# A fused spectral-attention and feed-forward kernel: the order of three steps in the first chunk, and ten of 48 weight blocks converted during attention

## The chip, the cores and the metric

The kernel runs on one core of one Trainium2 chip, as a single program. The metric is device time in microseconds (us), the median of several executions; beside it stands one execution recorded by the hardware profiler. Five engines work side by side, each with its own queue in order: TensorE (PE), VectorE (DVE), ScalarE (ACT), GpSimd (POOL) and SyncE (SP), which here issues all transfers.

## The reference

Sigmoid attention over 8 batches, 12 heads, 448 positions and 64 channels, then a spectral mix and a feed-forward block:

```python
scores = scale * np.matmul(q, k.transpose(0, 1, 3, 2)) - np.log(S)
attn = 1.0 / (1.0 + np.exp(-scores))
x = np.matmul(attn, v)                      # (8, 448, 768) after regrouping the heads
mixed = np.real(np.fft.fft(np.fft.fft(x, axis=1), axis=2)).astype(np.float32)
u = x + mixed
un = (u - mu) / np.sqrt(var + 1e-06)        # mean and variance of each row of u
ch = np.maximum(un @ w_ch1, 0.0) @ w_ch2    # 768 -> 3072 -> 768
return (u + ch).astype(np.float32)
```

The two weight matrices arrive as float64. The kernel sees each number as two 32-bit words, a low and a high one.

## The kernel before

**Stages.** First comes attention with the spectral mix: 48 groups of four steps, 192 steps in all, which the loop from L518 takes two at a time, with a tail of a few more. Then the feed-forward block runs over seven chunks of 512 rows: chunk 0 and chunk 1 in the plain way (`up_proj`, `evac` and `down_proj`, L554 to L584), five more by a scheme with fewer multiplications, whose weights chunk 1 prepares (`combine`).

**Order.** The order of instructions on each engine is written out by hand. `pin()` (L453) chains every instruction to the one before it on the same engine, so each engine works strictly in the order in which the program issues.

**One iteration of attention** (two steps) issues: postponed small operations, two `scores` (PE, then the sigmoid on ACT), two `values` (PE; every fourth one ends with `xT`, DVE's copy out of PSUM), some units of the spectral mix on PE, and then, step by step, whatever `at(t, fn)` has filed under that step, in the order of filing. Filed are the folds of `xT` (on POOL, some on DVE), the loads of q, k and v, `cast` (POOL, L117) and `rest` (DVE, L122), which split q and k in two parts for the scores two iterations later, and the row normalisation `norm`. A group g has its `cast` at step 4g-4 and its `rest` at step 4g-3.

**The weights during attention.** The 48 blocks of the weights (24 of `w1`, 24 of `w2`, each 128 x 768 numbers, 768 KB) pass through once: `weight_load(n)` brings block n into one of three `wr` buffers, and `weight_max(n)` (L264, DVE) takes the largest magnitude. `when_w` holds the step of each block: block n at step 14 + n*156//48. At step 170 `weight_scales` makes the two scale factors `wsc` from them.

**The weights in the first chunk.** Each block is loaded again and prepared in five steps (`prep_w(i, f, n)`, `i` for the matrix, `f` for the block):

- n = 0: the load, 768 KB from `w_in`, into a `wr` buffer or one of two `spare` buffers (L389)
- n = 1: `Abs` of the high word, as float32, into `t`, a `wt` buffer (ACT, L398)
- n = 2: clamp (L400) and shift (L402), DVE
- n = 3: two ORs (L406 takes bits of the low word, L408 the sign) finish the float32 number in `t`, DVE; then `h`, the scaled high part in float16 (the copy, ACT, L416), and a store of `t` to `t_dram` (SP, L417), from where chunk 1's `combine` reads it
- n = 4: `l`, the low part, `t*scale - h` in float16 (DVE, L419)

`order` lists the blocks: three of `w1`, then one of `w2` and one of `w1` by turns; from block 6 on an even place is a `w1` block and an odd one a `w2` block. `prep_step(k, n)` is one quarter of slot k. Its four quarters issue: the loads that `loadable` allows and **the low part of block k-1**; `Abs` of block k+1; clamp and shift of block k; the ORs, the copy and the store of block k. In chunk 0 every f has two slots (6+2f and 7+2f), until slot 48 is through. Its order in the program:

```python
up_proj(c, f)                 # PE: 18 matmuls, 512 columns
...                           # first slot: four quarters of prep_step
evac(c, f)                    # ACT: hh = relu(psh), L567;  DVE: hl, L568
...                           # second slot
down_proj(*prev)              # PE: the f before, from its hh and hl
```

`psh`, `hh` and `hl` have two buffers each. The first blocks are prepared at the end of attention, three more slots while the last units of the mix run.

Of the kernel before, what the change touches and what calls it, by code (L numbers as in the profile page):

```python
# [9 lines left out]
F32 = mybir.dt.float32  # L10
F32R = mybir.dt.float32r
I32 = mybir.dt.int32
AF = mybir.ActivationFunctionType
ALU = mybir.AluOpType
# [9 lines left out]
DM = 768  # L24
# [3 lines left out]
NFC = DF // 128  # L28
# [26 lines left out]
HI_MIN = 1.125 * 2.0 ** -15  # L55
HI_MAX = 2.0 ** 16 * 1.875 - 2.0 ** -7


def spectral_attention_ffn(tc, q, k, v, w1, w2, cd, cs, ident_in, out):
    nc = tc.nc  # L60
# [7 lines left out]
    with ExitStack() as top:  # L68
# [3 lines left out]
        t_dram = dram.tile([2, NP, 128, 2, DM], F32, name="t_dram")  # L72
# [8 lines left out]
        wpre = top.enter_context(tc.tile_pool(name="wpre", bufs=1))  # L81
# [6 lines left out]
        if True:  # L88
# [164 lines left out]
            wtile = {}  # L253
# [8 lines left out]
            def weight_max(n):  # L262
# [2 lines left out]
                    out=wmax[:, i, f:f + 1], in_=wtile.pop(n)[:, :, 1].bitcast(F32), op=ALU.max, axis=AX.X,  # L265
                    apply_absolute_value=True)

            def weight_scales():
                wm = cpool.tile([128, 2], F32, name="wm")
                nc.vector.tensor_reduce(out=wm, in_=wmax, op=ALU.max, axis=AX.X)  # L270
                ws = cpool.tile([128, 4], F32, name="ws")
                nc.gpsimd.partition_all_reduce(ws[:, 0:2], wm, 128, bass_isa.ReduceOp.absmax)

                wi = ws.bitcast(I32)
                nc.vector.tensor_scalar(
                    out=wi[:, 0:2], in0=wi[:, 0:2], scalar1=20, scalar2=0x7FF,
                    op0=ALU.logical_shift_right, op1=ALU.bitwise_and)
                nc.vector.tensor_scalar(
                    out=wi[:, 0:2], in0=wi[:, 0:2], scalar1=1023 - 60, scalar2=1023 + 60, op0=ALU.max, op1=ALU.min)
                nc.vector.tensor_scalar(  # L280
                    out=wi[:, 0:2], in0=wi[:, 0:2], scalar1=-896, scalar2=1 << 23, op0=ALU.add, op1=ALU.mult)
                nc.vector.reciprocal(ws[:, 2:4], ws[:, 0:2])
                nc.vector.tensor_scalar(
                    out=wsc[:, 0:1], in0=ws[:, 2:3], scalar1=2.0 ** 3, scalar2=None, op0=ALU.mult)
                nc.vector.tensor_scalar(
                    out=wsc[:, 1:2], in0=ws[:, 3:4], scalar1=2.0 ** 11, scalar2=None, op0=ALU.mult)
                nc.vector.tensor_scalar(
                    out=wsc[:, 2:3], in0=ws[:, 0:1], scalar1=ws[:, 1:2],
                    scalar2=2.0 ** -14 / UN_SCALE, op0=ALU.mult, op1=ALU.mult)
# [72 lines left out]
                return sorted(res, key=lambda x: x[0])  # L362

            prep = {}
            order = [(0, f) for f in range(NPRE)]
            for f in range(NFC):
                order += [(1, f)] + [(0, f + NPRE)] * (f + NPRE < NFC)
# [3 lines left out]
            def in_spare(k):  # L371
                return k >= 8 and k % 5 > 2

            def loadable(k, done):

                here = [j for j in range(k) if in_spare(j) == in_spare(k)]
                n = 2 if in_spare(k) else 3
                return len(here) < n or here[-n] < done

            def prep_w(i, f, n):  # L380

                if n == 0:
                    k = order.index((i, f))
                    if in_spare(k):
                        r = spare[0][:, k % 5 - 3]
                    else:
                        r = wpre.tile([128, DM, 2], I32, tag="wr", name="wr", bufs=3)
                    prep[i, f] = r
                    nc.sync.dma_start(  # L389
                        r.rearrange("p n w -> p (n w)"), (w1, w2)[i][:, f * 2 * DM:(f + 1) * 2 * DM])  # L390
                    return
                if n == 1:
                    prep[i, f] = prep[i, f], wpre.tile([128, DM], F32, tag="wt", name="wt", bufs=3)
                r, t = prep[i, f]
                ti = t.bitcast(I32)
                lo, hi = r[:, :, 0], r[:, :, 1]
                if n == 1:
                    nc.scalar.activation(t, hi.bitcast(F32), AF.Abs)  # L398
                elif n == 2:
                    nc.vector.tensor_scalar(  # L400
                        out=t, in0=t, scalar1=HI_MIN, scalar2=HI_MAX, op0=ALU.max, op1=ALU.min)
                    nc.vector.tensor_scalar(  # L402
                        out=ti, in0=ti, scalar1=3, scalar2=0x3FFFFFF8,
                        op0=ALU.logical_shift_left, op1=ALU.bitwise_and)
                elif n == 3:
                    nc.vector.scalar_tensor_tensor(  # L406
                        out=ti, in0=lo, scalar=29, in1=ti, op0=ALU.logical_shift_right, op1=ALU.bitwise_or)
                    nc.vector.scalar_tensor_tensor(  # L408
                        out=ti, in0=hi, scalar=-0x40000000, in1=ti, op0=ALU.bitwise_and, op1=ALU.bitwise_or)
                if n >= 3:  # L410
                    h, l = (x[f] for x in ((w1h, w1l), (w2h, w2l))[i])
                    if i == 0:
                        h, l = (x.rearrange("p c f -> p (c f)") for x in (h, l))
                    sc = wsc[:, i:i + 1]
                if n == 3:
                    nc.scalar.activation(h, t, AF.Copy, scale=sc)  # L416
                    nc.sync.dma_start(t_dram[i, f // 2][:, 1 - f % 2], t)  # L417
                elif n == 4:
                    nc.vector.scalar_tensor_tensor(  # L419
                        out=l, in0=t, scalar=sc, in1=h, op0=ALU.mult, op1=ALU.subtract)  # L420

            def prep_step(k, n):

                loads = []
                for d in range(2, 5):
                    if not loadable(k + d, k):
                        break
                    loads.append((d, 0))
                for d, m in ((*loads, (-1, 4)), ((1, 1),), ((0, 2),), ((0, 3),))[n]:
                    if k + d < len(order) and (k + d, m) not in prepped:  # L430
                        prepped.add((k + d, m))
                        prep_w(*order[k + d], m)
# [47 lines left out]
            when_w = {}  # L480
# [3 lines left out]

            def at(t, fn):
                extra.setdefault(t, []).append(fn)

            for b in range(B):
                for r, when in enumerate(FOLDS):
                    for n, t in enumerate(when):  # L490
                        e = nc.vector if r == 2 and n % 2 else nc.gpsimd
                        at(24 * b + LAG + t, lambda b=b, r=r, n=n, e=e: fold(b, r, n, e))
                at(24 * b + 27 + LAG, lambda b=b: units.extend(mix_units(b)))
            for gg in range(2, GG):
                at(8 * gg - 8 + LAG, lambda n=gg: load_v(n))
# [7 lines left out]
            at(9, lambda: nc.sync.dma_start(ident, ident_in))  # L503
            at(10, lambda: weight_load(1))
            at(TP, weight_scales)
            prepped = set()
            for e in range(NPRE + 2):
                for n, d in enumerate((0, 5, 6, 7, 9)):
                    if TP + 4 * e + d < TQ + LAG + 2 and (n < 4 or e < NPRE) and (n == 0 or e < NPRE + (n == 1)):
                        prepped.add((e, n))  # L510
                        at(TP + 4 * e + d, lambda e=e, n=n: prep_w(*order[e], n))
# [29 lines left out]
        with ExitStack() as fast, ExitStack() as st, ExitStack() as early:  # L541
# [72 lines left out]
            slot, step, m = NPRE, 0, 0  # L614
            while units or act_next or dve_next or sp_next:
                mix_rest(0.65)
                if len(units) < MIX_UP and m < NCC:
                    up_proj(0, 1, range(m, m + 1))
                    m += 1
                n = step % MIX_STEP  # L620
                if n < 4 and slot < NPRE + 2 * NW2:
                    prep_step(slot, n)
                    slot += n == 3
                step += 1
                pin()
# [99 lines left out]
            for j in range(NFC):  # L725
                f = 1 + j - (j > 4) - (j > 8) - (j > 12) - (j > 16)
# [168 lines left out]
            for c in range(NPLAIN + 1, NCK):  # L895
                t = (c - NPLAIN - 1) * NQ * NU
# [3 lines left out]
            for g in range(NGR):  # L900
                t = g * NU
# [81 lines left out]
```

## Time and profile before

| what | us |
|---|---|
| median of 3 runs | 1801.37 |
| lowest and highest run | 1796.43, 1805.48 |
| the profiled execution | 1796.9 |
| its span in the profile | 1795.1 |
| PE busy, all in all | 1671.5 |
| DVE busy | 1290.0 |
| ACT busy | 602.4 |
| POOL busy | 194.3 |

Attention takes the time to about 450 us, the end of the mix and chunk 0's blocks that to 718 us, chunk 0 and chunk 1 together that to about 945 us, and the five other chunks the rest. A row of a group reads: line, engine, operation, result <- inputs, shape, xcount | busy us, mean ns of one | idle us of the engine just before, and who ended it. A row of the timeline gives start, length and the instruction, with the idle time before it in brackets. `<-ACT hh L567` says that the engine waited until ACT had written `hh`.

### The profile page before, as it was taken

To read this page: it belongs to the slowest core of one execution; us is meant where nothing else is said; L and a number is where in the kernel's file an instruction comes from. 1 tells how busy PE (TensorE), PEld (TensorE's weight loads), DVE (VectorE), ACT (ScalarE), POOL (GpSimd) and SP (SyncE) were. 2 spreads that over 40 slices of the span, in tenths; PEclk is the share of its full clock that TensorE was granted. 3 is DMA by queue.
4 is the path that set the end of the run, shared out by engine and by line. 5 is a ranking of instruction groups with operands and counts; after the bars stand their busy time and mean duration, and the time that the engine had idled before them with its cause. 6 is when DMAs were issued, how large, how long until landed. Compare 5 with 4: busy or idle time off the path is not lost. (4 is left out here: it accounts for less than half of the span.)

```text
span 1795.1 us, 27673 instructions
## 1 busy us (share of the span) xinstructions
PE 1671.5 (93%) x10996; PEld 1070.2 (60%) x10996; DVE 1290.0 (72%) x2481; ACT 602.4 (34%) x767; POOL 194.3 (11%) x220
## 2 busy tenths in 40 slices
PE   8999999987878777999799999999999999999997
PEld 3555555543533333545357777777777777777774
DVE  3545577656777777467755888888888887888668
ACT  4444444434333333123232322333233323233221
POOL 4434444334000000000000000000000000000000
PEclk9999999998988999999999999999999999999999
DMA  7666767654666664587887466656475656566561
GB/s 234 209 213 211 237 208 240 212 177 118 225 211 211 211 211 140 192 307 278 302 288 271 186 247 234 238 214 242 175 277 206 237 199 254 215 229 241 216 227 59
DMA packets 109139, 394.95 MB, mean 220 GB/s; under 512 B 23521, under 2 KB 49362, under 8 KB 93522
## 3 DMA queue, kind: packets, MB, share of 16 engines
q1 hardware_dynamic: 109010, 393.19, 62.2%
q8 instruction: 86, 1.41, 0.3%
q14 instruction: 43, 0.35, 0.1%
HBM read 316.08 MB, written 73.92 MB: 217 GB/s over the span
## 5 line engine op out<-in xcount | busy, mean ns | idle before, releaser
L841 PE MATMUL pso<-ws,H 128*128 128x384 f16 x2520 | 422.6, 326 | 0.9 <-DVE H L796 0.8
L790 PE MATMUL psf<-ut,ws 128*128 128x256 f16 x3780 | 422.1, 273 | 1.1 <-DVE ur L600 1.1
L790 PEld LDWEIGHTS <-ws 128*128 128x128 f16 x3780 | 369.9, 98 | 50.3 <-issue 1.4
L841 PEld LDWEIGHTS <-H 128*128 128x128 f16 x2520 | 246.4, 98 | 155.8 <-DVE H L796 1.1
L136 ACT ACTIVATE a<-sc 112x900 f32<-112x900 f32 x192 | 166.6, 917 | 156.3 <-PE sc L132 156.1
L850 DVE TENSOR_TENSOR acc<-pso,acc 128x384 f32<-128x384 f32 x350 | 181.9, 550 | 19.0 <-PE pso L841 19.0
L579 PE MATMUL po<-w2h,hh 128*128 128x512 f16 (+1 forms) x384 | 133.7, 348 | 55.5 <-ACT hh L567 54.8
L152 PE MATMUL av<-a,vr 112*64 112x450 f32 x768 | 172.9, 573 | 3.7 <-DVE xT L161 3.7
L815 ACT ACTIVATE F<-F 128x1024 f32<-128x1024 f32 x60 | 63.5, 1058 | 332.0 <-DVE F L796 332.0
L796 DVE TENSOR_TENSOR H<-F,H 128x1024 f16<-128x1024 f32 x120 | 129.5, 1087 | 46.8 <-ACT H L825 46.8
L560 PE MATMUL psh<-ut,w1h 128*128 128x512 f16 x504 | 151.1, 382 | 5.0 <-DVE hl L568 5.0
L579 PEld LDWEIGHTS <-hh 128*128 128x128 f16 x768 | 77.5, 103 | 114.7 <-ACT hh L567 66.0
L579 PE MATMUL po<-w2h,hl 128*128 128x512 f16 (+1 forms) x384 | 132.9, 346 | 3.8 <-DVE hl L568 1.5
L796 DVE TENSOR_TENSOR F<-X,psf 128x256 f32<-128x256 f32 x240 | 98.0, 418 | 51.1 <-PE psf L790 48.1
L579 PE MATMUL po<-w2l,hh 128*128 128x512 f16 (+1 forms) x384 | 133.0, 346 | 0.0
L161 DVE TENSOR_SCALAR xT<-av 128x450 f32<-128x450 f32 x48 | 30.1, 626 | 141.8 <-PE av L152 141.8
L825 ACT ACTIVATE H<-F 128x1792 f16<-128x1792 f32 x60 | 101.8, 1697 | 89.0 <-DVE F L796 89.0
L796 DVE TENSOR_TENSOR F<-F 128x256 f32<-128x256 f32 x240 | 91.2, 421 | 17.7 <-ACT F L815 13.7
L568 DVE SCALAR_TENSOR_TENSOR hl<-psh,hh 128x512 f16<-128x512 f32 x48 | 33.2, 691 | 98.2 <-ACT hh L567 98.1
L132 PE MATMUL sc<-qh,kh 64*112 64x450 f32 x384 | 82.1, 423 | 19.7 <-ACT a L136 10.3
L152 PEld LDWEIGHTS av<-a,vr 112*64 112x64 f32 x768 | 47.8, 139 | 82.9 <-issue 68.3
L560 PE MATMUL psh<-ut,w1l 128*128 128x512 f16 x252 | 96.2, 382 | 0.0
(92 smaller groups left out, 1954.2 us busy)
## 6 DMA issues: line engine op xcount, KB each, us to landing
ws<-w_dram SPq DMA_DIRECT2D x120, 1344.0 KB, 5.9
wr<-w_in SPq DMA_DIRECT2D x80, 768.0 KB, 4.7
t_dram<-wt SPq DMA_DIRECT2D x48, 384.0 KB, 2.3
cb<-t_dram SPq DMA_DIRECT2D x24, 768.0 KB, 5.5
spare<-w_in SPq DMA_DIRECT2D x16, 768.0 KB, 4.6
qr<-q_in SPq DMA_DIRECT2D x48, 225.0 KB, 3.8
kr<-k_in SPq DMA_DIRECT2D x48, 224.0 KB, 3.5
vr<-v_in SPq DMA_DIRECT2D x24, 448.0 KB
```

What stands on the lines that cost most here:

```text
L132: nc.tensor.matmul(ps[:CP, j, :SQ], split[g, 1, kn][h, c * CP:(c + 1) * CP], split[g, 0, qn][h], start=(n == 0), stop=(n == 2))
L136: nc.scalar.activation(a, ps[:CP, :, :SQ], AF.Sigmoid, bias=-math.log(S), scale=1.0 / math.sqrt(D))
L152: nc.tensor.matmul(ps[j * D:(j + 1) * D, :SQ], vr[:, c, h * D:(h + 1) * D], a[:, j], start=(c == 0), stop=(c == 3))
L560: nc.tensor.matmul(hs[c, f], l[f][:, m], r[:, m], start=(m == n == 0), stop=(m == NCC - 1 and n == 2))
L568: nc.vector.scalar_tensor_tensor(out=hl, in0=ps, scalar=0.0, in1=hh, op0=ALU.max, op1=ALU.subtract)
L579: nc.tensor.matmul(po[n][:, at:at + hi - lo], l[:, cols], r[f][:, lo:hi], start=(f == 0 and m == 0 and at == 0), stop=(f == NFC - 1 and m ...
L790: nc.tensor.matmul(ps[:, :TH], w[:, x, a, m * 128:(m + 1) * 128], ut[y][:, b, m], start=(m == n == 0), stop=(m == n == 2))
L796: nc.vector.tensor_tensor(out=o, in0=x, in1=y, op=op)
L815: nc.scalar.activation(F[:, 0:4], F[:, 0:4], AF.Relu)
L825: nc.scalar.activation(hts[P][:, 0], F[:, 1:8], AF.Copy)
L841: nc.tensor.matmul(ps[:, :384], H[:, x, a, tp * 128:(tp + 1) * 128], w[:, y, b], start=(j == n == 0), stop=(j == 1 and n == 2))
L850: later(0, lambda: nc.vector.tensor_tensor(out=to, in0=ps[:, :384], in1=to, op=ALU.add))
```

## The change

The first part moves `(-1, 4)`, the low part of block k-1, from the first quarter of slot k to the third, behind clamp and shift of block k. The second part takes ten blocks (`ready`: `w1` blocks 7, 11, 15, 19, 23 and `w2` blocks 5, 9, 13, 17, 21) through `Abs`, clamp, shift and ORs during attention, in the three steps from the one in which their maximum is taken, and stores the float32 result in `t_dram`. In chunk 0 such a block is loaded from `t_dram` (384 KB) into the front of its buffer, and only the copy and the low part are left. As the low part of a ready block reads the loaded buffer itself, `loadable` counts that buffer as free one slot later, and `prep_step` looks for loads from one block ahead on instead of two. The ready blocks stand at the places 12 and 13, 20 and 21, 28 and 29, 36 and 37, 44 and 45 of `order`.

```diff
+            def to_float32(r, t, n):
+                ti = t.bitcast(I32)
+                lo, hi = r[:, :, 0], r[:, :, 1]
+                if n == 1:
+                    nc.scalar.activation(t, hi.bitcast(F32), AF.Abs)
+                elif n == 2:
...
+            def convert(n, k):
+                i, f = divmod(n, NFC)
+                if k == 1:
+                    made32[n] = wtile[n], wpre.tile([128, DM], F32, tag="wt", name="t32", bufs=3)
+                to_float32(*made32[n], k)
+                if k == 3:
+                    nc.sync.dma_start(t_dram[i, f // 2][:, 1 - f % 2], made32.pop(n)[1])
...
+            ready = {(i, f) for i in range(2) for f in range(7 - 2 * i, NFC, 4)}
...
-                return len(here) < n or here[-n] < done
+                return len(here) < n or here[-n] < done - (order[here[-n]] in ready)
...
+                    if (i, f) in ready:
+                        prep[i, f] = None, r.rearrange("p n w -> p (n w)")[:, :DM].bitcast(F32)
+                        nc.sync.dma_start(prep[i, f][1], t_dram[i, f // 2][:, 1 - f % 2])
+                        return
...
-                if n == 1:
+                if n == 1 and (i, f) not in ready:
...
+                if n < 4 and (i, f) not in ready:
+                    to_float32(r, t, n)
...
-                    nc.sync.dma_start(t_dram[i, f // 2][:, 1 - f % 2], t)
+                    if (i, f) not in ready:
+                        nc.sync.dma_start(t_dram[i, f // 2][:, 1 - f % 2], t)
...
-                for d in range(2, 5):
-                    if not loadable(k + d, k):
+                for d in range(1, 5):
+                    if k + d < len(order) and (k + d, 0) not in prepped and not loadable(k + d, k):
                         break
                     loads.append((d, 0))
-                for d, m in ((*loads, (-1, 4)), ((1, 1),), ((0, 2),), ((0, 3),))[n]:
+                for d, m in (loads, ((1, 1),), ((0, 2), (-1, 4)), ((0, 3),))[n]:
...
+            for t, x in when_w.items():
+                for n in x:
+                    if divmod(n, NFC) in ready:
+                        for j in range(3):
+                            at(t + j, lambda n=n, j=j: convert(n, j + 1))
```

The last loop stands ahead of the other `at` calls, so within a step the conversion is issued first. The body of `to_float32` is the arithmetic of n = 1 to 3 of `prep_w`, unchanged.

More of the change, by code (lines that the diff above doesn't have):

```diff
@@ L266, in weight_max @@
                     apply_absolute_value=True)
+            def to_float32(r, t, n):
[4 more added lines that the diff above has]
+                elif n == 2:
+                    nc.vector.tensor_scalar(
+                        out=t, in0=t, scalar1=HI_MIN, scalar2=HI_MAX, op0=ALU.max, op1=ALU.min)
+                    nc.vector.tensor_scalar(
+                        out=ti, in0=ti, scalar1=3, scalar2=0x3FFFFFF8,
+                        op0=ALU.logical_shift_left, op1=ALU.bitwise_and)
+                else:
+                    nc.vector.scalar_tensor_tensor(
+                        out=ti, in0=lo, scalar=29, in1=ti, op0=ALU.logical_shift_right, op1=ALU.bitwise_or)
+                    nc.vector.scalar_tensor_tensor(
+                        out=ti, in0=hi, scalar=-0x40000000, in1=ti, op0=ALU.bitwise_and, op1=ALU.bitwise_or)
+            def convert(n, k):
[5 more added lines that the diff above has]
+                    nc.sync.dma_start(t_dram[i, f // 2][:, 1 - f % 2], made32.pop(n)[1])
+            made32 = {}
             def weight_scales():
@@ L391, in prep_w @@
                     return
-                if n == 1:
+                if n == 1 and (i, f) not in ready:
                     prep[i, f] = prep[i, f], wpre.tile([128, DM], F32, tag="wt", name="wt", bufs=3)
                 r, t = prep[i, f]
[L395 to L409, printed above, removed]
+                if n < 4 and (i, f) not in ready:
+                    to_float32(r, t, n)
                 if n >= 3:
```

## The prediction

> **What bounds the kernel now.** First the page: its span and the engines' busy shares in 40 slices of 44.9 us.
>
> ```profile
> span 1795.1 us, 27673 instructions
> PE   8999999987878777999799999999999999999997
> DVE  3545577656777777467755888888888887888668
> ```
>
> TensorE (PE) is full nearly everywhere except in the slices from about 400 to 720 us, where it shows 7 to 8 tenths. Three windows (PE, weight loads, DVE, ACT and POOL busy, then clock, DMA share and rate): attention, the first chunk, and what follows it.
>
> ```profile
> 36.00:445.00 409.00, 376.11 (x2246) 206.79 (x2244) 245.30 (x410) 178.59 (x226) 180.30 (x200) 0.97 0.64 207
> 500.00:718.00 218.00, 173.17 (x829) 82.61 (x828) 165.61 (x215) 75.45 (x96) 0.00 (x0) 0.93 0.58 195
> 719.00:760.00 41.00, 41.00 (x223) 21.59 (x221) 16.26 (x30) 6.73 (x8) 0.00 (x0) 1.00 0.52 188
> ```
>
> Attention is PE's: 376 of 409 us. In the first chunk nobody is full: PE 173 of 218, DVE 166. So the waits of that window come next.
>
> ```profile
> PE po L579 <- ACT hh L567: 42.8, 19, 3.0
> DVE hl L568 <- ACT hh L567: 28.2, 19, 1.5
> DVE w2l L419 <- ACT w2h L416: 20.1, 20, 1.1
> ```
>
> PE waits for `hh`, the evacuation of `psh`; DVE waits for ACT in two places, once per f each. One f in order of time, DVE and then ACT, shows a closed loop of the two:
>
> ```profile
> 571.79 1.02 DVE L419 SCALAR_TENSOR_TENSOR w2l<-wt,wsc,w2h 128x768 f16<-128x768 f32 x1 [1.00 <-ACT w2h L416]
> 572.72 0.56 DVE L400 TENSOR_SCALAR wt<-wt 128x768 f32<-128x768 f32 x1
> 573.31 0.56 DVE L402 TENSOR_SCALAR wt<-wt 128x768 int32<-128x768 int32 x1
> 573.91 0.96 DVE L406 SCALAR_TENSOR_TENSOR wt<-wr,wt 128x768 int32<-128x768 int32 x1
> 574.90 0.96 DVE L408 SCALAR_TENSOR_TENSOR wt<-wr,wt 128x768 int32<-128x768 int32 x1
> 577.35 0.69 DVE L568 SCALAR_TENSOR_TENSOR hl<-psh,hh 128x512 f16<-128x512 f32 x1 [1.49 <-ACT hh L567]
> 577.95 1.01 DVE L419 SCALAR_TENSOR_TENSOR w1l<-wt,wsc,w1h 128x768 f16<-128x768 f32 x1
> ...
> 583.02 1.02 DVE L419 SCALAR_TENSOR_TENSOR w2l<-wt,wsc,w2h 128x768 f16<-128x768 f32 x1 [1.00 <-ACT w2h L416]
> ```
>
> ```profile
> 575.90 0.93 ACT L416 ACTIVATE w1h<-wt,wsc 128x768 f16<-128x768 f32 x1 [3.33 <-DVE wt L408]
> 576.74 0.58 ACT L567 ACTIVATE hh<-psh 128x512 f16<-128x512 f32 x1
> 577.21 0.90 ACT L398 ACTIVATE wt<-spare 128x768 f32<-128x768 f32 x1
> ```
>
> A block costs DVE 4.07 us from start to end: low 0.93, clamp 0.59, shift 0.60, the two ORs 0.99 and 0.96. An f is two blocks, `hl` (0.60), 1.49 us until copy and `hh` are through, and 1.00 us until the other copy is: 8.14 + 0.60 + 1.49 + 1.00 = 11.23, which is 583.02 - 571.79. PE needs less, as the `hl` rows after the last block show:
>
> ```profile
> 728.75 0.69 DVE L568 SCALAR_TENSOR_TENSOR hl<-psh,hh 128x512 f16<-128x512 f32 x1 [7.03 <-ACT hh L567]
> 736.54 0.69 DVE L568 SCALAR_TENSOR_TENSOR hl<-psh,hh 128x512 f16<-128x512 f32 x1 [7.09 <-ACT hh L567]
> ```
>
> 7.79 us for an f: while blocks are prepared, 3.44 us of each f are DVE's, and what is taken off the loop comes off the kernel.
>
> **The low part moved.** It stands behind the next block's clamp and shift (1.19 us), so the copy (0.03 + 0.93) is done when DVE reaches it. The clamp needs that block's Abs, which ACT issued ahead of the copy (572.72 follows at once today). How many waits there are:
>
> ```profile
> L419 DVE SCALAR_TENSOR_TENSOR w2l<-wt,wsc,w2h 128x768 f16<-128x768 f32 x24 | 24.4, 1018 | 22.2 <-ACT w2h L416 22.1
> L419 DVE SCALAR_TENSOR_TENSOR w1l<-wt,wsc,w1h 128x768 f16<-128x768 f32 x21 | 21.2, 1008 | 1.0 <-ACT w1h L416 1.0
> ```
>
> Some 23 of 1.0 us. The last block has no successor and keeps its wait; ten belong to the ready pairs below; **12 x 1.0 = 12.0 us** go. The 1.49 us before `hl` stay: copy and `hh` still come after the ORs.
>
> **Ready blocks.** In `order` they are 12 and 13, 20 and 21, up to 44 and 45: both blocks of one f, five times. From the end of block 11's ORs to the end of block 14's DVE spends now 1.00 + 4.07 + 1.49 + 0.60 + 4.07 + 1.00 + 4.07 = 16.30. After: low 11 waits 1.00 for its copy (nothing is left to stand before it) and takes 0.93; `hl` starts at 0.03 + 0.84 + 0.84 + 0.58 + 0.03 = 2.32, as two copies and `hh` are in line on ACT; then `hl` 0.60, low 12 0.93, clamp and shift of 14 1.19, low 13 0.93, ORs 1.95: 7.92. **8.38 saved, five times: 41.9 us.** Next bound: the two `hl` intervals of a pair are 6.99 and 7.09, under PE's 7.79, so PE falls 1.5 us behind; the plain f's at 11.23 - 1.00 = 10.23 let it catch up 2.44 each. After the last pair the blocks are soon at their end, and about 1.4 of PE's lag stays: -1.4. **Chunk: 12.0 + 41.9 - 1.4 = 52.5 us.**
>
> Transfers there:
>
> ```profile
> wr<-w_in SPq DMA_DIRECT2D x80, 768.0 KB, 4.7
> t_dram<-wt SPq DMA_DIRECT2D x48, 384.0 KB, 2.3
> ```
>
> Ten loads halve and ten stores leave the chunk. A ready block's buffer is released one slot later (its low part reads it), so its successor is loaded later. The tightest is block 16: loaded in slot 12, right after block 11's store, with its Abs behind block 14's copy, which starts 7.9 us after those ORs: 8 us against 4.7. I cost it at nothing; without that cover it is at most the 4.7 us, five times.
>
> **What attention gets.** Ten times an Abs (0.90, ACT), clamp, shift and ORs (3.14, DVE), a store. DVE has room, and PE a reserve on the short path, `rest` to the scores that read `kl`:
>
> ```profile
> L161 DVE TENSOR_SCALAR xT<-av 128x450 f32<-128x450 f32 x39 | 24.4, 627 | 116.7 <-PE av L152 116.7
> 167.74 0.98 DVE L122 TENSOR_TENSOR kl<-kr,kh 128x448 fp32r<-128x448 f32 x1
> 171.56 0.46 PE L132 MATMUL sc<-qh,kh 64*112 64x450 f32 x2
> ```
>
> Before each `xT` DVE idles 3.0 us on average, and `kl` is 2.84 us early. But the conversions stand first in their slots. Slots 36, 88, 108, 160 put clamp and shift ahead of `rest`, 62 and 134 the ORs, 75 and 147 all four, 49 and 121 none. And these operations are longer while POOL works, as the three blocks turned at the end of attention show:
>
> ```profile
> 403.72 1.22 DVE L402 TENSOR_SCALAR wt<-wt 128x768 int32<-128x768 int32 x1
> 406.79 1.30 DVE L406 SCALAR_TENSOR_TENSOR wt<-wr,wt 128x768 int32<-128x768 int32 x1
> 408.13 1.62 DVE L408 SCALAR_TENSOR_TENSOR wt<-wr,wt 128x768 int32<-128x768 int32 x1
> ```
>
> With a clamp of 0.55 that block took 4.69 us. So: two blocks overrun the reserve by 4.69 - 2.84, 3.7 us; at slot 109 clamp and shift (1.8 stretched) delay `norm`'s scaling, whose ACT copy precedes two sigmoids, where PE waits already:
>
> ```profile
> 243.99 0.46 PE L132 MATMUL sc<-qh,kh 64*112 64x450 f32 x2 [0.60 <-ACT a L136]
> ```
>
> and 0.2 for each of the other seven: **7 us**. Bounds: 0, as work is only added, and 56 (ten times 4.69 + 0.90, all on the path); I stay near the reserve's row. On SP a store waits for the ORs; behind it stand the `kr`, `qr` and weight loads, needed five slots later, so nothing.
>
> The Trainium skill (SBUF — State Buffer, "Who interferes with whom") says more: a DVE instruction with two SBUF inputs, or in a two-port mode, and a GpSimd one that reads SBUF exclude each other for the whole instruction. The stretched rows agree, and the rule speaks against the move, from a stage without POOL work to one with 180 us of it; the rival "POOL in the way" is what it would make.
>
> **Sum.** Against the profiled execution (1796.9, span 1795.1): 1796.9 - 52.5 + 7.0 = 1751.4. The median of the runs is 4.5 above it, so 1801.4 - 45.5 = **1755.9**.
>
> **Rivals.**
> - *POOL in the way* (0.15). If each of the four operations is held as 403.72 was (0.66 longer), a block takes 5.8 us, and every one overruns: 10 x (5.8 - 2.84) = 30 us at most, 15 if half do: 1763.9 to 1778.9. For it: the stretched rows. Against: five of ten put two operations or none in the way.
> - *PE's clock* (0.10). PE was slow after a gap of 2.97 us, and not after 1.40:
>
> ```profile
> 577.37 0.39 PE L579 MATMUL po<-w2h,hh 128*128 128x512 f16 x1 [2.97 <-ACT hh L567]
> 578.09 0.61 PE L579 MATMUL po<-w2h,hl 128*128 128x512 f16 x1
> 588.59 0.39 PE L579 MATMUL po<-w2h,hh 128*128 128x512 f16 x1 [1.40 <-ACT hh L567]
> 589.32 0.39 PE L579 MATMUL po<-w2h,hl 128*128 128x512 f16 x1
> ```
>
>  If PE stays busy 173 us in what are then 218 - 52.5 = 165.5, it becomes the bound: 7.7 lost, 1763.6. Gaps of at most 2.44 speak against it.
> - *The wait only moves* (0.05): the clamp waits for Abs, or the low part still for the copy. The 12.0 don't come: 1767.9.
> - *Attention becomes DVE's* (0.03), slower than before: each conversion stops PE for its stretched 4.69 + 0.90, and its ORs hold POOL, which casts the next q and k, for another 1.9: 75 - 52.5 = 22 us, 1824. It decides from 5.25 us per block. DVE's 245 of 409 us, 292 with ten blocks, speak against it.
>
> The forecast has 0.67. Its own range is 1741 (no cost in attention, and the fastest run, 1796.4) to 1766 (twice the cost, slower runs); with half of the first rival the range is **1741 to 1776**. About 9 us (0.5%) is what a measurement here can tell from no change: faster 0.96, same 0.02, slower 0.02.
>
> **What would show it.** L419's waits in all drop from 24 us to about 7; five pairs of `hl` 7 us apart among others at 10.2; blocks end near 672 instead of 718 us; four conversion rows per block between 75 and 360 us, with PE idle under 1 us behind most. Wrong if PE idles over 2 us behind several conversions, if the copy of a ready block waits for its load, or if the plain f's stay at 11.2.

## The result, and the profile after

| | before | after |
|---|---|---|
| median, us | 1798.9 (four runs, 1791.77 to 1805.48) | 1745.91 (four runs, 1744.19 to 1746.7) |
| the profiled execution | 1796.9 | 1746.7 |

The ratio is 0.9705, with a 95% interval of 0.9665 to 0.9745: 53 us by the medians, 50.2 by the profiled executions. The forecast was 1755.9, 45.5 less than before.

The page of the changed kernel, span and busy shares in 40 slices, now of 43.6 us:

```profile
span 1744.9 us, 27688 instructions
PE   8999999997879999998899999999999999999997
DVE  4556677866788884768557888788878888887768
```

The run of 7s and 8s on PE has shrunk to a few slices. Attention and the first chunk as windows (PE, weight loads, DVE, ACT, POOL, then clock, DMA share, rate):

```profile
36.00:445.00 409.00, 375.86 (x2220) 205.80 (x2216) 281.62 (x446) 182.02 (x231) 183.39 (x196) 0.97 0.67 213
500.00:655.00 155.00, 147.41 (x760) 74.53 (x761) 127.26 (x168) 64.69 (x84) 0.00 (x0) 0.97 0.67 225
```

In attention DVE has 36.3 us more than before (245.30) and PE the same; in the chunk PE is 95% busy instead of 79%. Three of the chunk's waits (500 to 665 us: waiter, awaited, us, times, longest; ACT's waits for DVE's ORs, the other side of the loop, are left out):

```profile
DVE hl L597 <- ACT hh L596: 23.7, 20, 1.5
PE po L608 <- ACT hh L596: 11.7, 5, 5.1
DVE w2l L442 <- ACT w2h L438: 6.0, 6, 1.0
```

The wait of `w2l` fell from some 20 us to 6.0 in six cases: five pairs and the last block. `hl`'s wait of 1.49 stays. One pair and the f after it, DVE in order of time:

```profile
543.66 0.69 DVE L597 SCALAR_TENSOR_TENSOR hl<-psh,hh 128x512 f16<-128x512 f32 x1 [1.49 <-ACT hh L596]
544.26 0.55 DVE L275 TENSOR_SCALAR wt<-wt 128x768 f32<-128x768 f32 x1
544.85 0.56 DVE L277 TENSOR_SCALAR wt<-wt 128x768 int32<-128x768 int32 x1
545.32 1.01 DVE L442 SCALAR_TENSOR_TENSOR w1l<-wt,wsc,w1h 128x768 f16<-128x768 f32 x1
546.25 0.95 DVE L281 SCALAR_TENSOR_TENSOR wt<-spare,wt 128x768 int32<-128x768 int32 x1
547.24 0.96 DVE L283 SCALAR_TENSOR_TENSOR wt<-spare,wt 128x768 int32<-128x768 int32 x1
549.20 1.02 DVE L442 SCALAR_TENSOR_TENSOR w2l<-wt,wsc,w2h 128x768 f16<-128x768 f32 x1 [1.00 <-ACT w2h L438]
550.50 0.69 DVE L597 SCALAR_TENSOR_TENSOR hl<-psh,hh 128x512 f16<-128x512 f32 x1 [0.29 <-ACT hh L596]
551.11 1.01 DVE L442 SCALAR_TENSOR_TENSOR w1l<-wr,wsc,w1h 128x768 f16<-128x768 f32 x1
552.04 0.55 DVE L275 TENSOR_SCALAR wt<-wt 128x768 f32<-128x768 f32 x1
552.63 0.56 DVE L277 TENSOR_SCALAR wt<-wt 128x768 int32<-128x768 int32 x1
553.10 1.01 DVE L442 SCALAR_TENSOR_TENSOR w2l<-wr,wsc,w2h 128x768 f16<-128x768 f32 x1
554.03 0.95 DVE L281 SCALAR_TENSOR_TENSOR wt<-wr,wt 128x768 int32<-128x768 int32 x1
555.02 0.96 DVE L283 SCALAR_TENSOR_TENSOR wt<-wr,wt 128x768 int32<-128x768 int32 x1
557.46 0.69 DVE L597 SCALAR_TENSOR_TENSOR hl<-psh,hh 128x512 f16<-128x512 f32 x1 [1.49 <-ACT hh L596]
```

The reader sees the forecast's picture: low 11 (549.20) keeps its 1.00, `hl` finds `hh` 0.29 us away, low 12, clamp, shift, low 13 and the ORs follow without a gap. From the last OR of block 11 to that of block 14 it is 555.02 - 547.24 = 7.78 us (forecast 7.92, before 16.30). The pair's two `hl` intervals are 6.84 and 6.96; between plain f's the trace has 9.90 to 9.91.

Where the 50.2 us went is read from rows that both traces have: the first `hl` of chunk 0, the last low part, and an `hl` behind the last block (728.75 before, in the prediction). Before:

```profile
463.15 0.69 DVE L568 SCALAR_TENSOR_TENSOR hl<-psh,hh 128x512 f16<-128x512 f32 x1 [1.63 <-ACT hh L567]
717.70 1.02 DVE L419 SCALAR_TENSOR_TENSOR w2l<-wt,wsc,w2h 128x768 f16<-128x768 f32 x1 [1.00 <-ACT w2h L416]
```

After:

```profile
466.36 0.69 DVE L597 SCALAR_TENSOR_TENSOR hl<-psh,hh 128x512 f16<-128x512 f32 x1 [1.62 <-ACT hh L596]
663.84 1.02 DVE L442 SCALAR_TENSOR_TENSOR w2l<-wt,wsc,w2h 128x768 f16<-128x768 f32 x1 [1.00 <-ACT w2h L438]
678.47 0.69 DVE L597 SCALAR_TENSOR_TENSOR hl<-psh,hh 128x512 f16<-128x512 f32 x1 [7.03 <-ACT hh L596]
```

| | forecast | measured |
|---|---|---|
| up to the first `hl` | +7.0 | 466.36 - 463.15 = +3.2 |
| the chunk, from there to the `hl` behind the last block | -52.5 | (678.47 - 466.36) - (728.75 - 463.15) = -53.5 |
| from there to the end | 0 | +0.1 |

### The profile page after: what moved, and what is told of

Same layout as the page of the kernel before. It is cut to its first block, busy times and chain, and to the rows that moved or that the text cites. A ratio compares the mean times of both kernels' runs of the same rounds, so it can differ in the third digit from the quotient of the medians.

```text
span 1744.9 us, 27688 instructions
## 1 busy us (share of the span) xinstructions
PE 1659.8 (95%) x10996; PEld 1070.3 (61%) x10996; DVE 1296.0 (74%) x2481; ACT 601.7 (34%) x767; POOL 201.8 (12%) x220
## 5 line engine op out<-in xcount | busy, mean ns | idle before, releaser
L608 PE MATMUL po<-w2h,hh 128*128 128x512 f16 (+1 forms) x384 | 128.9, 336 | 19.0 <-ACT hh L596 16.3
L608 PE MATMUL po<-w2h,hl 128*128 128x512 f16 (+1 forms) x384 | 128.5, 335 | 1.0
L608 PE MATMUL po<-w2l,hh 128*128 128x512 f16 (+1 forms) x384 | 128.5, 335 | 0.0
```

What stands on the lines that cost most here:

```text
L608: nc.tensor.matmul(po[n][:, at:at + hi - lo], l[:, cols], r[f][:, lo:hi], start=(f == 0 and m == 0 and at == 0), stop=(f == NFC - 1 and m ...
```

## The experiments

All start from the changed kernel; ratios are to the kernel before on the same chip. The theory: the chunk is the closed loop of DVE and ACT, both parts shorten it, and attention pays a few us. The main rivals: attention's price is much larger and hidden in the sum, or one of the two parts gives nothing.

**The low part alone** (`e1_low`): no ready blocks and no conversions.

```diff
-            ready = {(i, f) for i in range(2) for f in range(7 - 2 * i, NFC, 4)}
+            ready = set()
```

> The first part of the change alone: the low part behind the next block's clamp and shift, no ready blocks. Loop theory (the first chunk is set by DVE and ACT in turn, so whatever leaves that loop leaves the kernel): an f takes 9.91 us, as the plain f's of the changed kernel do, instead of 11.23, 21 times, so 28 us less than before, about 1771. By the price on record alone (1.00 us for each of 22 waits): 22 us less, 1777. Rival, the wait only moves: under 8 us less, above 1791. Attention stays as it was; its cold-clock windows (half of PE's clock) come or do not come without any conversion.

Measured: 1768.95 us, ratio 0.9837 (0.9802 to 0.9873), 27.2 us less than before. Two of its chunk's waits (500 to 690 us):

```profile
DVE hl L597 <- ACT hh L596: 28.2, 19, 1.5
PE po L608 <- ACT hh L596: 25.1, 16, 1.7
```

No wait of a low part is left but the last block's, and every f takes 9.90 to 9.91 us, 1.32 less than 11.23: the wait of 1.00, and 0.32 that the forecast didn't have.

**The ready blocks alone** (`e2_ready`): the low part at its old place, first in its slot.

```diff
-                for d, m in (loads, ((1, 1),), ((0, 2), (-1, 4)), ((0, 3),))[n]:
+                for d, m in ((*loads, (-1, 4)), ((1, 1),), ((0, 2),), ((0, 3),))[n]:
```

> The second part alone: ten ready blocks, the low part first in its slot as before. Loop theory: plain f's stay at 11.23, a pair of hl intervals takes about 15 (one more wait of 1.00 than in the changed kernel); 40 us less in the chunk, some 3 to 6 back in attention: 1762 to 1766. Both savings together would then be 28 + 40 = 68 against 53.5 in the changed kernel: ten of the waits are counted twice, and PE is the bound at the end. Rival, ready blocks do nearly all of it: within 5 us of the changed kernel, below 1751.

Measured: 1764.36, ratio 0.982 (0.979 to 0.985), 31.8 less; in its profile the span is 37.3 less. The low part waits as before the change, once for each `w2` block that is prepared in the chunk (500 to 680 us):

```profile
DVE w2l L442 <- ACT w2h L438: 15.1, 15, 1.1
```

Plain f's are at 11.22 to 11.23, pairs at 6.98 + 7.17. From landmarks in the traces the parts alone give 27.6 and 39.0 us in the chunk, 66.6 together; the whole change gives 53.5. The difference of 13.1 is overlap. 12.2 of it are there at the last low part: ten of the waits that e1 removes belong to the pairs, where five go with the ready `w2` blocks in e2 as well and five stay, ahead of a pair, in the whole change. The rest is PE, which falls behind further when both are in.

**The conversions alone** (`e3_conv`): as e1, but attention still turns the ten blocks and stores them; nobody reads them.

```diff
+            ready = set()
+            turned = {(i, f) for i in range(2) for f in range(7 - 2 * i, NFC, 4)}
...
-                    if divmod(n, NFC) in ready:
+                    if divmod(n, NFC) in turned:
```

> Conversions in attention that nobody uses: the first chunk prepares all 48 blocks as without ready blocks (low part moved); the ten float32 blocks are stored twice. Against the kernel with the low part moved alone this is the price of the conversions. Theory A (they cost PE little by themselves, 2 to 3 us; the rest of the 9 us by which attention fell behind in the changed kernel's trace were half-clock windows after gaps of PE that were there before): 2 to 4 us more, with zero to four half-clock windows between 40 and 380 us. Theory B (conversions bring the half-clock windows): 8 to 10 us more, four such windows at the same places, near 102, 157, 246 and 273 us.

Measured: 1772.34, ratio 0.9872 (0.984 to 0.9905): over e1 3.4 us by the medians and 6.3 by the ratios, with intervals that overlap. Its profiled execution, the longest of the four (1779.66), has what theory B asked for: the first `hl` comes 9.0 us later than in e1 (474.63 and 465.67), and the clock is lowered near 100, 160, 250 and 275 us. But 3.7 of the 9.0 are there at step 36, ahead of any conversion, and e1 and e4, which convert nothing, have four such stretches as well (near 100, 155, 270 and 320 us). What the conversions add step by step is 4.4 us (below, under attention), nearer to theory A than to B; the times alone don't decide it.

**The ready blocks for nothing** (`e4_free`): no conversions; the ten blocks are loaded from one place of `t_dram`, and all 48 are stored in the chunk.

```diff
-                        nc.sync.dma_start(prep[i, f][1], t_dram[i, f // 2][:, 1 - f % 2])
+                        nc.sync.dma_start(prep[i, f][1], t_dram[0, 0][:, 1 - f % 2])
...
-                    if divmod(n, NFC) in ready:
+                    if False:
```

> Ready blocks without conversions: no conversion in attention; in the first chunk the ten blocks are loaded from another block's float32 numbers, so ten of 48 blocks hold wrong weights, and are stored again. The gain without its price. Loop theory: hl intervals as in the changed kernel (9.91, 6.85, 6.95), the chunk 53 us shorter. Theory A: 2 to 4 us faster than the changed kernel, 1742 to 1744. Theory B: 8 to 10 us faster, 1736 to 1738, and no half-clock window between 40 and 380 us.

Measured: 1742.84, ratio 0.9699 (0.967 to 0.9728), beside the changed kernel's 0.9705. The `hl` intervals are those of the changed kernel, so the ten extra stores in the chunk cost nothing, and the conversions cost 3.1 us by the medians and about 1 by the ratios, or 5 by the ratio of the changed kernel's repeat (`r0_after`, below). The intervals don't put it more exactly.

**The evacuation ahead of the copy** (`e5_evac`, with the changed kernel again as `r0_after` beside it). What is left of the loop is `hl`'s 1.49: the copy (0.84) and `hh` stand behind the ORs. Here `evac` is issued before the last quarter of the first slot: `hh` before the copy, `hl` before the ORs.

```diff
                             for step in range(4):
+                                if step == 3 and n == 0 and f:
+                                    evac(c, f)
                                 prep_step(slot, step)
                             slot += 1
+                            continue
```

> The changed kernel again, on the chip of the three runs beside it: 1742 to 1748 if the first measurement holds. Its half-clock windows in attention: if they hang on the moment at which a gap falls and not on the conversions, some of the four (near 102, 157, 246 and 273 us) are missing or stand elsewhere.

> The changed kernel with the evacuation of psh issued ahead of the third block step's ORs and copy, in place of behind them: hh then stands before the copy on ACT, and hl before the ORs on DVE. Loop theory: the 1.49 us in front of hl go, a plain f takes DVE 8.42 us and a group of four 28.9, less than PE's 31.2, so PE is the bound and every hl interval is 7.79: 21 of them are 163.6 against 170.7 in the changed kernel, 7 us less, 1737 to 1740. Rival, ACT or PE held up by something else (hl now waits in DVE's queue for PE, and the ORs behind it are late): within 2 us of the changed kernel.

Measured: r0 1747.38, ratio 0.9728 (0.9711 to 0.9746); e5 1730.93, ratio 0.9639 (0.9622 to 0.9656), 16.4 us under r0, against 7 to 10 expected. The chunk, and two `hl` in a row, in e5:

```profile
500.00:655.00 155.00, 155.00 (x833) 81.34 (x832) 133.84 (x175) 68.64 (x89) 0.00 (x0) 1.00 0.72 248
```

```profile
526.32 0.69 DVE L597 SCALAR_TENSOR_TENSOR hl<-psh,hh 128x512 f16<-128x512 f32 x1 [0.28 <-ACT hh L596]
535.05 0.69 DVE L597 SCALAR_TENSOR_TENSOR hl<-psh,hh 128x512 f16<-128x512 f32 x1 [0.27 <-ACT hh L596]
```

The wait is 0.27 instead of 1.49, a plain f takes DVE 8.73, and PE is full: the bound is now PE, which it wasn't in the changed kernel. PE begins an f every 7.79 us (526.08, 533.87, 541.65); four f's with a pair in them are 29.35 us apart by their `hl` at first and 31.1 later, when `hl` has caught up with PE's 4 x 7.79. Between the second `hl` and the last but one, e5 takes 158.5 us and r0 169.0. I had reckoned 21 f's of 7.79, 163.6, as the least for that stretch, and that floor was too high: the second `hl` came 11.4 us behind the matmuls it reads (485.54, 496.93) and the late one 0.7 (654.69, 655.41), so PE had done part of that work before the stretch began. By the profiles (span 1728.7 against 1742.6) 11.9 of 13.9 us are gained up to that late `hl`; the 2.0 behind it I didn't settle.

**The same without ready blocks** (`e6_evac_low`): e5 with `ready = set()`.

> The same without ready blocks and conversions: low part behind clamp and shift, evacuation early, all 48 blocks prepared in the first chunk. Loop theory: DVE's 8.42 us per f is still more than PE's 7.79, so intervals are 8.42; against the low part alone (9.91) 19 intervals save 28 us, less 3 to 4 that PE is behind at the end: 25 us, about 1744. What ready blocks are still worth is then about 5 to 10 us in place of 42.

Measured: 1745.51, ratio 0.9725 (0.9707 to 0.9743), as fast as the changed kernel, without a conversion in attention. Its chunk:

```profile
500.00:655.00 155.00, 144.22 (x748) 70.03 (x746) 147.72 (x197) 70.78 (x90) 0.00 (x0) 1.00 0.78 265
```

DVE is 95% busy: the loop is gone and DVE itself is the bound, at 8.72 to 8.73 us an f. The ready blocks take work from it: worth 14.6 us now (1745.51 - 1730.93; 5 to 10 were expected), where on top of the moved low part alone they were worth 23.0 (1768.95 - 1745.91, from two sets of runs; 24 by the ratios).

**The conversion last in its step** (`e7_last`): the loop that files the conversions stands behind the other `at` calls.

```diff
-            for t, x in when_w.items():
-                for n in x:
-                    if divmod(n, NFC) in ready:
-                        for j in range(3):
-                            at(t + j, lambda n=n, j=j: convert(n, j + 1))
...
+            for t, x in when_w.items():
...
             for t in range(0, TQ + LAG + 4, 2):
```

> The changed kernel with the conversions filed last in their steps in place of first, so behind the q and k rests, the folds and norm's scaling of the same step. If the place in front of norm's scaling (step 109) makes the 3.0 us by which attention falls behind there, the gap of 2.13 us in front of the scores near 246 us goes back to 0.60 and there is no half-clock window at it; the other conversions cost nothing either way. In all 1 to 3 us less than the changed kernel, since attention's last 70 us take back part of any delay. Rival, the sheer DVE time of a conversion makes it: no difference in the gap.

Measured: 1744.58, ratio 0.9712 (0.9693 to 0.9732), 2.8 under r0, with intervals that overlap. The trace shows where: one gap of PE. After:

```profile
245.82 0.53 PE L132 MATMUL sc<-qh,kh 64*112 64x450 f32 x2 [2.13 <-ACT a L136]
...
240.00:250.00 10.00, 7.87 (x44) 4.14 (x40) 7.71 (x11) 5.32 (x7) 1.58 (x2) 0.83 0.34 81
```

And e7:

```profile
244.18 0.46 PE L132 MATMUL sc<-qh,kh 64*112 64x450 f32 x2 [0.61 <-ACT a L136]
...
240.00:250.00 10.00, 9.39 (x58) 5.15 (x56) 9.93 (x14) 6.12 (x9) 2.77 (x4) 1.00 0.51 135
```

With clamp and shift behind `norm`'s scaling the gap is back at 0.6 us, as before the change (0.60), and the clock in that window is 1.00 instead of 0.83.

**Both** (`e8_evac_last`: e5's and e7's edits; `r1_evac` is e5 again, beside it).

> The changed kernel with the early evacuation again, beside its variant: 1729 to 1733 if the first measurement holds.

> Early evacuation and conversions filed last in their steps, together. The two work in different stages, so the gains should add: 0 to 3 us less than early evacuation alone, 1728 to 1731, with no 3.0 us step in attention at the norm's scaling (xT of step 112), and hl intervals as with early evacuation alone.

Measured: r1 1733.38, ratio 0.9626 (0.9611 to 0.9641); e8 **1728.23**, ratio 0.9600 (0.9582 to 0.9619), the lowest of all. 5.1 under r1, more than the 0 to 3 expected; the intervals meet. e8's trace shows the gap at 245 us gone, as e7's does; what the rest is stays open.

## Why the prediction was right

**The loop** was the bound, and both parts shorten it, as e1 and e2 show each by itself. The term "Chunk" came out at 53.5 for 52.5, with two small errors of opposite sign in it. Each plain f saved 1.32 and not 1.00: I took an operation's distance to the next as fixed, but the moved low part stands between shift and OR, and the last section has the rows. The two intervals of a pair take 13.80 instead of 22.45, 8.65 less where I had 8.38. So DVE is through its blocks 57.1 us sooner, counted from the first `hl` to the last low part (254.55 - 197.48; the forecast's 12.0 + 41.9 is 53.9). PE's lag behind the last pair is then larger, 57.1 - 53.5 = 3.6 where I had 1.4.

**Attention** is the mis-sized term: 7 us, measured 3.2 up to the first `hl`, and that holds luck. I compared the starts of `xT` step by step. At step 36, ahead of any conversion, the changed kernel is already 3.2 us ahead, since PE ran at a lowered clock at 30 to 40 us in the profiled execution of before (0.66 there, 1.00 after). These steps appear in each trace with conversions first in their steps (after, e2, e3, r0, e5, r1) and in none without conversions (e1, e4, e6): +3.0 at 108, +0.75 at 134, +0.3 at 88 and at 160, +0.1 at 147, nothing at 36, 49, 62, 75 and 121. Their sum is 4.4. Three stretches at a lowered clock near 100, 155 and 270 us, which the profiled execution of before doesn't have, cost the changed kernel another 4.7: -3.2 + 4.4 + 4.7 = 5.9, and it stands 6.1 behind at step 164. The tail of attention takes 2.9 of that back. It does so in r0 and e2 too, but not in e3, e5 and r1; how much of the 4.4 reaches the chunk thus differs from execution to execution, and why stays open.

Within the 7, the forecast's 3.7 for the two blocks that overrun the reserve was wrong, and 1.8 for `norm` too little. The block at step 75, DVE and POOL of the changed kernel:

```profile
166.58 0.55 DVE L275 TENSOR_SCALAR t<-t 128x768 f32<-128x768 f32 x1
167.16 0.56 DVE L277 TENSOR_SCALAR t<-t 128x768 int32<-128x768 int32 x1
167.64 0.99 DVE L181 TENSOR_TENSOR xp<-fd 128x452 f32<-128x452 f32 x1
168.55 1.30 DVE L281 SCALAR_TENSOR_TENSOR t<-wr,t 128x768 int32<-128x768 int32 x1
169.89 0.96 DVE L283 SCALAR_TENSOR_TENSOR t<-wr,t 128x768 int32<-128x768 int32 x1
170.76 0.62 DVE L122 TENSOR_TENSOR ql<-qr,qh 128x450 fp32r<-128x450 f32 x1
171.30 0.62 DVE L122 TENSOR_TENSOR kl<-kr,kh 128x448 fp32r<-128x448 f32 x1
```

```profile
167.49 0.66 POOL L117 TENSOR_SCALAR qh<-qr 128x450 fp32r<-128x450 f32 x1 [4.44 <-PE sc L132]
168.12 0.93 POOL L117 TENSOR_SCALAR kh<-kr 128x448 fp32r<-128x448 f32 x1
```

POOL works from 167.49 to 169.05. Only one of the four operations starts in that time (the shift, under way when it begins, keeps its 0.56), so the block takes 3.37 us of DVE and not 4.69; and `ql` and `kl`, pushed behind it, take 0.62 each where `kl` took 0.98 before. The delay pays for part of itself, and the scores get `kl` in time. The price moved to `norm`: there the gap ahead of the scores grew from 0.60 to 2.13, and PE ran the next stretch at a lower clock, which the forecast didn't have: it had counted gaps up to 2.44 us as an argument against that. e7 shows it by undoing it. Of the signs of being wrong, PE idle for over 2 us behind a conversion thus came once, not several times.

**The rest of the 10 us** between 1755.9 and 1745.9 is no step of the working: by the profiled executions the forecast is 4.7 off, 1.0 in the chunk and 3.8 up to it; the other 5.3 is how the medians stand to them, 4.5 above for before as I had it, 0.8 below for after. The lower end of the forecast's range doesn't follow from its terms: 1796.4 - 52.5 is 1743.9 and not 1741; the measured median lies above both.

**The rivals.** *POOL in the way* fell as a price, not as a mechanism. The ten conversions as groups:

```profile
L275 DVE TENSOR_SCALAR t<-t 128x768 f32<-128x768 f32 x10 | 6.3, 631 | 3.3 <-ACT t L273 3.3
L277 DVE TENSOR_SCALAR t<-t 128x768 int32<-128x768 int32 x10 | 6.9, 693 | 0.3
L281 DVE SCALAR_TENSOR_TENSOR t<-wr,t 128x768 int32<-128x768 int32 x10 | 12.3, 1229 | 0.0
L283 DVE SCALAR_TENSOR_TENSOR t<-wr,t 128x768 int32<-128x768 int32 x10 | 13.7, 1373 | 0.3
```

A block takes 3.93 us on average against 0.55 + 0.56 + 0.95 + 0.96 = 3.02 in the chunk, where POOL is idle. Most of the 39.3 us in all found room: the steps above sum to 4.4. The Trainium skill (SBUF — State Buffer, "Who interferes with whom") has the port pair of DVE and GpSimd as an exclusive lock; the rows of step 75 agree, 1.30 for an OR beside POOL and 0.96 for the next without it. *PE's clock* didn't bind: 147.41 us busy of 155 at 0.97. *The wait only moves* fell, with 6.0 us left at L442. *Attention becomes DVE's* fell, with 281.62 us of 409. Transfers cost nothing in the chunk: the full list of its waits (500 to 665 us) holds none for a transfer.

## What to carry to other kernels

Where two engines wait for each other in turn and neither is full, follow one round of the loop and ask what the awaited instruction is queued behind: here letting `hh` and `hl` pass one copy and two ORs gave, by the ratios of e1 and e6, (0.9837 - 0.9725) x 1796 = 20 us, nearly the 24 that moving ten blocks of work to another stage gave, and both together more. Once the loop is open, the next bound (DVE in e6, PE in e5) says what the moved work is worth, and it is less than it was in the loop. Work added to a stage with room still belongs behind what the critical engine waits for in the same step.

## What the hardware showed unexpectedly

**The distance to the next operation depends on whether it needs this one.** So the rows here have it; no run changes that alone. In the timeline of the pair above the shift starts 0.59 us after the clamp that it depends on (544.26, 544.85); in the prediction's rows the OR comes 0.60 after its shift (573.31, 573.91); but the low part, which is independent, starts 0.47 after the shift (544.85, 545.32), and where the dependent second OR starts 0.99 after the first (546.25, 547.24), an independent clamp behind an OR starts 0.88 after it, in e5:

```profile
527.91 0.96 DVE L283 SCALAR_TENSOR_TENSOR wt<-wr,wt 128x768 int32<-128x768 int32 x1
528.79 0.55 DVE L275 TENSOR_SCALAR wt<-wt 128x768 f32<-128x768 f32 x1
```

The low part between shift and OR thus saves some 0.1 each time, and the clamp right behind the ORs too.

**The same gap of PE is followed by a low clock in one execution and not in another.** One pair of rows from the changed kernel, and the same place in its repeat r0:

```profile
101.24 0.59 PE L226 MATMUL psx<-ident,xT 128*112 128x128 f32 x3 [2.74 <-DVE u L233]
103.52 3.00 PE L152 MATMUL av<-a,vr 112*64 112x450 f32 x8
```

```profile
103.59 0.59 PE L226 MATMUL psx<-ident,xT 128*112 128x128 f32 x3 [2.74 <-DVE u L233]
105.53 1.73 PE L152 MATMUL av<-a,vr 112*64 112x450 f32 x8
```

The same eight matmuls take 3.00 us or 1.73. Every trace, with and without conversions, has five gaps in which PE waits for DVE's `u`: 2.74 us near 100 and 270, 2.10 near 157 and 326, 1.88 near 213. The clock is lowered behind the first four in varying choice (in e4 behind all four), behind the 1.88 in none. The gap of 2.13 near 245 stands in the six traces with conversions first in their steps, and the clock is lowered behind it in each. Near 31 us it took less: gaps of 1.48 and 0.87 in a row in before, of 0.84 and 0.87 in r0, with the clock at 0.66 and 0.83 from 30 to 40 us. Each of the later stretches costs 1.4 to 2.9 us in the starts of `xT`, mostly 1.5, which is as much as several of the differences measured here and a reason to compare step by step. The Trainium skill (TensorE: Matmul & The Clock Gate, "What's actually happening") has the clock decided in free-running windows of some 3.4 us, so that the point of change depends on where in the window the work lands. That the same gap came out both ways agrees. The gap that its "Why this matters for your kernels" has one avoid is one of over some 3 us; here gaps of 2.13 and 2.74 us were followed by a low clock.
